# Attention and a two-layer MLP on one core: weight pieces in attention decoded like the others, decoding spread, omega loaded first, layer 2's first sums placed earlier

## The chip, the cores and the metric

The kernel runs on one core of a Trainium2 chip. A core has five engines with a queue of instructions each: TensorE (PE in the profile, with its weight loads as PEld), VectorE (DVE), ScalarE (ACT), GpSimd (POOL) and SyncE (SP), which here only issues DMAs. The metric is the device time of one execution in microseconds (us), the median of several. Lower is better.

## The reference

Inputs are float32 after drawing, but U, V and the two weight matrices come as float64, eight bytes a number.

```python
q_s, k_s = q * scale, k * scale                      # (8, 8, 576, 64), scale = 64 ** -0.25
def phi(x):
    proj = einsum('bhsd,md->bhsm', x, omega)         # omega (128, 64)
    h = proj - sum(x * x, -1, keepdims=True) / 2
    h = h - max(h, -1, keepdims=True)
    return exp(h) / sqrt(128)
kv  = einsum('bhsm,bhsd->bhmd', phi(k_s), v);  z = sum(phi(k_s), 2)
num = einsum('bhsm,bhmd->bhsd', phi(q_s), kv)
den = einsum('bhsm,bhm->bhs', phi(q_s), z) + 1e-6
x = (num / den) as (8, 576, 512)
u = x + ((x^T @ U) @ V)^T                            # mixing over the sequence, rank 32
out = u + relu(u @ w_ch1) @ w_ch2                    # 512 -> 2048 -> 512
```

## The kernel before, in words

Products need nearly full float32 precision, so an operand is split into a high and a low half in float32r (`xh`/`xl`, `wh`/`wl`, `uh`/`ul`, `gh`/`gl`), and three matmuls make one product: high by high, high by low, low by high. The high half is a cast on ACT, the low one a subtraction on DVE or POOL.

**Attention** is a loop of 16 rounds with nine steps each, one step for each tile of 128 positions. A round handles keys of one pair of heads and queries of another at once. A step's stages are delayed against each other over loop iterations (the dictionary DELAY): transposing 384 columns every third step (`xT`, L611, DVE), high and low halves (L615 ACT, L619 POOL), the projection with omega into `p_p` (L738 to L740, PE), the negated maximum `nm` (L746, DVE, one per step), the exponential `e` (L753, ACT, four per step), for keys the sum `p_kv` (L650), for queries a transpose `p_q` (L676), its copy `eT` (L681, in turns on DVE and ACT), the product `p_n` with the keys' sum (L696), and the division (L706 to L721, DVE). Finished sequences go through `mixing`, one piece of which is run twice per loop iteration; it writes `u` to DRAM.

**Decoding.** In the same loop a generator, `decoding`, turns float64 into float32. A piece is 128 rows of up to 512 numbers: a DMA brings the two words of each number into `raw` (two buffers, SP, L192 for weights), ACT takes the magnitude of the high word (L132), and DVE does the rest in slots, one for each call of the generator: clamp (L150), shift (L151) and sign (L154). For the low word there are two ways. The first `lean` pieces take two more DVE slots (L157, L158) that make a correction `de`, which POOL adds in float32 (L176). Later pieces have ACT round the low word to an integer `low` (L135), which POOL adds to the bits (L171). `lean` is EARLY = 11 pieces: U, two of V and eight of the first weight matrix, which is all that the loop decodes but the beginning of a twelfth; `left` allows the loop 64 calls. The loop calls the generator in two of three iterations. At a piece's last slot the next magnitude and a further load are issued. What is done with a decoded piece (`rest`: sums, casts, low halves) is spread over the next piece's slots.

**The MLP** uses Strassen-like products with seven multiplications (S1 to S4 are the sums of the left operand, T1 to T4 of the right one). Layer 1 goes over nine chunks of 512 rows and four weight groups `g`; `unit` does one chunk by one group, seven products `i` of 12 matmuls each (L954). Its results are added on DVE (L942), passed through ACT's relu (L938) and stored to DRAM by SP (L932). An accumulator bank is used again by a later product, so that one waits for the addition that empties the bank. In the last chunk, layer 2's weights are split beside (`w2_ops`, L505 on ACT, L509 on DVE and POOL), and the first left operand of layer 2, `acts[0] = Step(0)`, is prepared: its load (L1130, 1 MB), sums (`value`, L1145; S1 and S3 on POOL, S2 and S4 on DVE) and splits (`split`, L1171 on ACT and L1178 on DVE). S1 to S4 stand in the products 0 to 3 of group 3.

**Layer 2** takes 36 steps of 84 matmuls (L1331). After the first product of its step 0, the pools `up` and `dec` are closed and their memory becomes the pool `vp`, in the order in which its tiles are first asked for: `gh` and `gl` (nine buffers each), then `graw`, which `Step(1)` loads. A tile waits for those readers and writers whose place it takes. Step 1 starts only when all of its seven operands are there (`now.need(6 if n else i)`).

**Order.** Instructions that go through `K` (`keep_in_program_order`) keep the program's order on their engine; that holds for decoding's DVE slots and ACT passes, for the additions of `unit`, and for sums and splits. The others, DMA issues and most of attention's instructions among them, are put in order by the framework's planner, which follows data and a model of the durations. An engine then runs its queue strictly in that order, so a waiting instruction holds up all behind it.

Of the kernel before, what the change touches and what calls it, by code (L numbers as in the profile page):

```python
# [9 lines left out]
F32 = mybir.dt.float32  # L10
F32R = mybir.dt.float32r
U32 = mybir.dt.uint32
I32 = mybir.dt.int32
AF = mybir.ActivationFunctionType
ALU = mybir.AluOpType
# [14 lines left out]
def performer_mlp_kernel(ctx: ExitStack, tc, q, k, v, omega, U, V, w1, w2, out):  # L30
# [7 lines left out]
    nc = tc.nc  # L38
    B, H, S, D = q.shape
# [3 lines left out]
    P = 128  # L43
    NP = B // 2
    NU = H // 2
    NT = 9
# [7 lines left out]
    scale = float(D) ** -0.25  # L54
# [3 lines left out]
    K = tc.keep_in_program_order  # L58
# [26 lines left out]
    warm = const.tile([P, 1], F32, name="warm")  # L85
# [27 lines left out]
            return outer[n // 2][:, n % 2]  # L113
        return dec.tile([P, PIECE, 2], U32, name="raw", bufs=RB)

    def decoding(jobs, late, lean, base, hold=(), defer=()):


        raws, mags, lows = {}, {}, {}
        fetched = [0]  # L120

        def fetch(i):
            while fetched[0] < min(i, len(jobs)):
                j = fetched[0]
                raws[j] = raw_place(j, base)[:, : jobs[j][1], :]
                jobs[j][0](raws[j])
                fetched[0] += 1

        def magnitude(i):
            if i < len(jobs):  # L130
                mags[i] = jobs[i][2]()
                K(nc.scalar.activation(out=mags[i], in_=f32(raws[i][:, :, 1]), func=AF.Abs))  # L132
                if i >= lean:
                    lows[i] = dec.tile([P, PIECE], I32, name="low", tag="de", bufs=2)[:, : jobs[i][1]]
                    K(nc.scalar.activation(out=lows[i], in_=raws[i][:, :, 0], func=AF.Copy, scale=2.0**-29))  # L135

        fetch(depth())
        for _ in range(late):
            yield
        magnitude(0)  # L140
        rest = []
        for i, job in enumerate(jobs):
            n = job[1]
            raw, m = raws.pop(i), mags.pop(i)
            low, high = raw[:, :, 0], raw[:, :, 1]
            e = lows.pop(i) if i in lows else dec.tile([P, PIECE], F32, name="de", bufs=2)[:, :n]


            slots = [
                lambda: nc.vector.tensor_scalar(m, m, _LEAST, _MOST, ALU.max, ALU.min),  # L150
                lambda: nc.vector.tensor_scalar(  # L151
                    words(m), words(m), 3, 0x3FFFFFFF, ALU.logical_shift_left, ALU.bitwise_and
                ),
                lambda: nc.vector.scalar_tensor_tensor(  # L154
                    words(m), high, 0xC0000000, words(m), ALU.bitwise_and, ALU.bitwise_or
                ),
                lambda: nc.vector.tensor_scalar(words(e), words(m), 0xFF800000, None, ALU.bitwise_and),  # L157
                lambda: nc.vector.scalar_tensor_tensor(e, low, 2.0**-52, e, ALU.mult, ALU.mult),  # L158
            ]
            if i >= lean:  # L160
                slots = slots[:3]
            for j, slot in enumerate(slots):
                tc.keep_in_program_order(slot())
                for _ in range(-(-len(rest) // (len(slots) - j))):
                    rest.pop(0)()
                if j == len(slots) - 1 and i not in hold and i not in defer:
                    magnitude(i + 1)
                if j == len(slots) - 1:
                    fetch(i + 1 + depth())
                    if i >= lean:  # L170
                        nc.gpsimd.tensor_tensor(out=m.bitcast(I32), in0=m.bitcast(I32), in1=e, op=ALU.add)  # L171
                yield
            if i in defer:
                magnitude(i + 1)
            if i < lean:
                nc.gpsimd.tensor_tensor(out=m, in0=m, in1=e, op=ALU.add)  # L176
            rest = [lambda fn=fn, m=m: fn(m) for fn in job[3:]]
            if i in hold:
                while rest:
                    rest.pop(0)()  # L180
                    yield
                magnitude(i + 1)
        while rest:
            rest.pop(0)()
            yield
# [128 lines left out]
    def weight_jobs():  # L314
        for g in range(NG):
            yield from w1_jobs(g)
# [55 lines left out]
    EARLY = 1 + 2 + 4 * EARLY_GROUPS  # L372
# [154 lines left out]
    late = {}  # L527
# [53 lines left out]
        spare[:, n : n + 4 * D1].rearrange("p (h b d) -> p h b d", h=2, b=2),  # L581
    ))

    def blocks(src, raw, unit, j):


        pair, hp = unit
        for h in range(2):
            for a in range(2):
                r = h * D + a * BLK  # L590
                nc.sync.dma_start(
                    out=raw[r : r + BLK, j * S : (j + 1) * S].rearrange("i (b c) -> i b c", c=BLK),
                    in_=src[2 * pair + j, 2 * hp + h, :, a * BLK : (a + 1) * BLK].rearrange("(b i) c -> i b c", i=BLK),
                )

    class Part:
# [4 lines left out]
            self.raw = io.tile([P, 2 * S], F32, name=("kt", "qt")[place])  # L601
            self.xh, self.xl = [], []

        def load(self, j):
            blocks(self.src, self.raw, self.unit, j)

        def turn(self):

# [163 lines left out]
    units = [(pair, hp) for pair in range(NP) for hp in range(NU)]  # L772
    keys = [Keys(i, i) for i in range(2)]
    rounds = {0: list(keys)}
    for j in range(2):
        for p in keys:
            p.load(j)
    nc.vector.memset(warm, 0.0)
    nc.scalar.activation(out=warm, in_=warm, func=AF.Exp)

    nc.vector.memset(idle, 0.0)
    for _ in range(12):
        nc.tensor.matmul(ps.tile([P, P], F32, name="p_m", tag="p_m"), idle, idle, start=True, stop=True)
    om = mp.tile([P, 2, D], F32, name="om", tag="y", bufs=2)
    for j in range(2):
        nc.gpsimd.dma_start(out=om[:, j, :], in_=omega)
    make_identity(nc, ident)
    for vt, vm in values:

# [8 lines left out]
    nc.vector.memset(f32(omh), 0.0)  # L798
    nc.vector.memset(f32(oml), 0.0)
    nc.vector.memset(f32(svm), 0.0)  # L800
    nc.vector.tensor_scalar_mul(om, om, scale)
    pom = ps.tile([P, P], F32, name="p_q", tag="p_q", bufs=2)
    nc.tensor.transpose(pom, om.rearrange("p j d -> p (j d)"), ident)
    for j in range(2):
# [10 lines left out]
        "project": 2, "use0": 4, "peak": 3, "combine": 6,  # L815
    }
    steps = {}
    decoder = decoding([u_job(), *v_jobs(), *weight_jobs()], 6, EARLY, -EARLY, defer=(EARLY + 3,))
    mixers = []
    x = None  # L820
    for s in range(NR * NT + 7):
# [28 lines left out]
        at = lambda op: steps.get(s - DELAY[op])  # L850
        for p in at("turn0").group(0) if at("turn0") else []:
            p.turn()
        if s % 3:
            advance(decoder)
        st = at("copy")
        for p in st.queries() if st else []:
# [331 lines left out]
    for n in range(2, len(order)):  # L1188
        c, g = order[n]
        if n == 2:  # L1190
            widen()
        if g == 0:
            while nxt and nxt.step():
                pass
        if n == 4:
            nxt = rights[2] = prepare(2, temps=None)
        elif g == 0 and 1 < c < NCH - 1:
            nxt = rights[c + 1] = prepare(c + 1)
        if n == 6:
            both(nxt)  # L1200
        if n in (6, 7):
            continue
        right = guest if c == 1 else rights[c]
        leaving = n >= 6 and g == NG - 1
        if c == NCH - 1:
            if g == 0:
                for _ in second:
                    pass
                prepare_w2(0)
                prepare_w2(1)  # L1210
                for _ in range(4):
                    w2_ops[0].step(-1)
            if g == 1:
                acts[0] = Step(0)
        for i in unit(c, g, right, banks(n + 1)):
            chores(n, i)
            if c == NCH - 1:
                if g:
                    w2_ops[g - 1].step()
                w2_ops[g].step(i)  # L1220
                w2_ops[g].step(i)
                if i == 2 and 1 < g + 1 < NG:
                    prepare_w2(g + 1)
                if g + 1 < NG and i > 2 + (g > 0):
                    w2_ops[g + 1].step(-1)
                if g + 1 < NG and i == 6:
                    w2_ops[g + 1].step(-1)
                if g == 2 and i % 2:
                    acts[0].split(len(acts[0].ops))
                if g == 2 and i == 6:  # L1230
                    acts[0].need(2)
                if g == 3 and i < 4:
                    acts[0].value(("S1", "S2", "S3", "S4")[i])
            elif nxt:
                for _ in range(2 if leaving else 1):
                    nxt.step(i if leaving else -1)
# [74 lines left out]
    for n in range(NS):  # L1311
# [9 lines left out]
        for i in range(PRODUCTS):  # L1321
# [14 lines left out]
            if n == 0:  # L1336
                if i == 0:
                    while w2_ops[NG - 1].step():
                        pass
                    phase.close()  # L1340
                    decodes.close()
                    late["vp"] = ctx.enter_context(tc.tile_pool(name="vp", reuse_waits="tile", bufs=1))
                    now.split(3)
                    now.split(4)
                    acts[1] = Step(1)
                else:
                    for _ in range(1 + (i > 2)):
                        step = now if len(now.ops) < PRODUCTS else acts[1]
                        if len(step.ops) < PRODUCTS:
                            step.split(len(step.ops))  # L1350
                        if len(now.ops) == PRODUCTS:
                            now.need(6)
            elif n + 1 < NS:
                acts[n + 1].split(i)
# [42 lines left out]
```

## Time and profile before

| | |
|---|---|
| median of 3 runs | 1077.48 us (1076.21 to 1078.4) |
| profiled execution | 1082.14 us, span 1080.4 us, mean granted clock 0.989 |
| PE busy | 1043.0 us, 97% of the span |
| DVE, ACT, POOL busy | 883.6, 611.7, 511.2 us |
| attention | to about 330 us |
| layer 1 | about 336 to 715 us |
| layer 2 | from about 715 us |

A row such as "L746 DVE TENSOR_REDUCE nm<-p_p 128x4 f32<-128x512 f32 x91 | 61.5, 677 | 5.6 <-ACT e L753 2.6" reads: line 746 of the kernel, engine and operation, output and inputs by the program's names, shapes, how many; busy time in us, mean duration in ns; idle time of the engine just before them, and what ended it. In the rows of waits stand the total in us, the number and the longest. In the rows of stretches stand start and end, length, the busy time of PE, PEld, DVE, ACT and POOL (with instructions), the granted PE clock, the busy share of the DMA engines and GB/s. In the timeline the first two numbers are start and duration, and in brackets stands the idle time before, with what ended it. Durations of matmuls include their way through the array; back to back they start every 0.12 us at full clock.

### The profile page before, as it was taken

Reading aid. Unit: us, or ns where it says so; the run is one execution under the profiler, and the core shown is the slowest. Engines: PE = TensorE matmul, PEld = TensorE weight load, DVE = VectorE, ACT = ScalarE, POOL = GpSimd, SP = SyncE. Lnnn points to the kernel's source line nnn. Section 1 sums busy time; section 2 is a strip of 40 time slices with the busy share of each in tenths; the row PEclk is TensorE's granted clock in tenths of the full one; section 3 lists DMA queues with packets and bytes.
Section 4 is the critical chain, followed back from the end, with each engine's and each line's share of the span. In section 5 each row is a group of like instructions: output and inputs, shape, how many; then the busy total and the mean of one; then the engine's idle time right before and its main releaser. Section 6 shows DMA issues by size and latency. Waiting matters only on the chain. (4 is left out here: it accounts for less than half of the span.)

```text
span 1080.4 us, 23909 instructions
## 1 busy us (share of the span) xinstructions
PE 1043.0 (97%) x8497; PEld 1016.6 (94%) x8497; DVE 883.6 (82%) x1531; ACT 611.7 (57%) x1468; POOL 511.2 (47%) x455
## 2 busy tenths in 40 slices
PE   8999999999998889999999999989999999999998
PEld 7898888889987789999999999989999999999998
DVE  3899899988898966666677576669999999999995
ACT  4888878879874545445345354654444444444442
POOL 3446878856433623223323414445744545535543
PEclk8999999999999989999999999999999999999999
DMA  7779587576335764877778856964445455355451
GB/s 129 139 147 167 104 194 156 108 178 121 87 89 127 200 172 114 231 223 176 190 186 194 223 166 200 314 208 141 173 169 166 144 175 167 128 176 167 132 174 47
DMA packets 380408, 175.55 MB, mean 162 GB/s; under 512 B 275553, under 2 KB 353377, under 8 KB 375681
## 3 DMA queue, kind: packets, MB, share of 16 engines
q1 hardware_dynamic: 380224, 173.97, 60.9%
q8 instruction: 67, 1.10, 0.4%
q14 instruction: 53, 0.43, 0.1%
q0 software_dynamic: 64, 0.07, 0.0%
HBM read 110.00 MB, written 63.96 MB: 161 GB/s over the span
## 5 line engine op out<-in xcount | busy, mean ns | idle before, releaser
L753 ACT ACTIVATE e<-p_p,nm 128x128 f32<-128x128 f32 x576 | 166.4, 388 | 34.0 <-DVE nm L746 22.9
L1145 POOL TENSOR_TENSOR gs<-graw 128x512 f32<-128x512 f32 x70 | 104.0, 1489 | 146.5 <-DMA graw<-g 93.8
L1171 ACT CAST gh<-gs 128x512 fp32r<-128x512 f32 x140 | 86.6, 621 | 152.5 <-DVE gs L1145 76.4
L938 ACT ACTIVATE g<-g 128x512 f32<-128x512 f32 x105 | 66.4, 632 | 170.7 <-DVE g L942 93.6
L619 POOL TENSOR_TENSOR xl<-xT,xh 128x384 fp32r<-128x384 f32 x96 | 101.9, 1078 | 112.2 <-ACT xh L615 97.5
L1178 DVE TENSOR_TENSOR gl<-gs,gh 128x512 fp32r<-128x512 f32 x140 | 138.0, 994 | 15.9 <-ACT gh L1171 14.1
L746 DVE TENSOR_REDUCE nm<-p_p 128x4 f32<-128x512 f32 x144 | 97.7, 680 | 20.6 <-PE p_p L740 10.3
L171 POOL TENSOR_TENSOR wf<-wf,low 128x512 int32<-128x512 int32 x24 | 32.4, 1349 | 135.7 <-ACT g L938 123.4
L738 PE MATMUL p_p<-omh,xh 128*128 128x256 f32 x288 | 93.4, 324 | 1.6 <-ACT e L753 1.3
L1256 POOL TENSOR_TENSOR u<-u,p 128x256 f32<-128x256 f32 x72 | 74.8, 1067 | 33.8 <-DVE u L1256 31.2
L1178 DVE TENSOR_TENSOR gl<-graw,gh 128x512 fp32r<-128x512 f32 x107 | 80.7, 769 | 8.9 <-ACT gh L1171 7.8
L1171 ACT CAST gh<-graw 128x512 fp32r<-128x512 f32 x107 | 63.9, 620 | 41.6 <-PE p_p L1331 9.2
L740 PE MATMUL p_p<-omh,xl 128*128 128x256 f32 x288 | 82.3, 286 | 0.1
L696 PE MATMUL p_n<-kv,eT 128*128 128x65 f32 x512 | 74.8, 274 | 7.5 <-DVE eT L681 3.1
L739 PE MATMUL p_p<-oml,xh 128*128 128x256 f32 x288 | 81.9, 284 | 0.0
L1331 PE MATMUL p_p<-wh,gh 128*128 128x256 f32 x288 | 81.1, 282 | 0.0
L1331 PE MATMUL p_p<-wh,gl 128*128 128x256 f32 x288 | 81.0, 281 | 0.0
L1331 PE MATMUL p_p<-wl,gh 128*128 128x256 f32 x288 | 80.9, 281 | 0.0
L696 PEld LDWEIGHTS p_n<-kv,eT 128*128 128x128 f32 x512 | 68.3, 194 | 12.9 <-DVE eT L681 5.5
L1331 PE MATMUL p_q<-wh,gl 128*128 128x256 f32 x276 | 77.7, 282 | 0.8 <-DVE gl L1178 0.8
L1331 PE MATMUL p_q<-wh,gh 128*128 128x256 f32 x276 | 77.8, 282 | 0.4 <-ACT gh L1171 0.4
L954 PE MATMUL p_n<-uh,wh 128*128 128x256 f32 x256 | 73.3, 286 | 4.6 <-DVE g L942 4.5
(271 smaller groups left out, 4058.6 us busy)
## 6 DMA issues: line engine op xcount, KB each, us to landing
graw<-g SPq DMA_DIRECT2D x36, 1024.0 KB, 5.2
g<-g SPq DMA_DIRECT2D x282, 128.0 KB, 2.4
raw<-in_moe_w_ch_dram SPq DMA_DIRECT2D x22, 512.0 KB, 4.7
u_dram<-ut SPq DMA_DIRECT2D x36, 256.0 KB, 2.4
u<-u_dram SPq DMA_DIRECT2D x36, 256.0 KB, 2.6
out_dram<-u SPq DMA_DIRECT2D x36, 256.0 KB, 2.9
kt<-in_k_dram SPq DMA_DIRECT2D x120, 72.0 KB, 2.7
qt<-in_q_dram SPq DMA_DIRECT2D x120, 72.0 KB, 2.7
```

Source lines behind the costliest of these rows:

```text
L619: nc.gpsimd.tensor_tensor(out=self.xl[-1], in0=self.turned, in1=f32(self.xh[-1]), op=ALU.subtract)
L696: nc.tensor.matmul(pn[:, h, :], eT[:, h, :], kv[:, h, s // 5, :], start=True, stop=True)
L738: nc.tensor.matmul(o, part.xh[g][:, ts], oh, start=True, stop=False)
L739: nc.tensor.matmul(o, part.xh[g][:, ts], ol, start=False, stop=False)
L740: nc.tensor.matmul(o, part.xl[g][:, ts], oh, start=False, stop=True)
L746: nc.vector.tensor_reduce(out=self.nm[:, :n], in_=self.pp[:, :n], axis=AX.X, op=ALU.max, negate=True)
L753: nc.scalar.activation(out=self.e[:, j, :], in_=self.pp[:, j, :], func=AF.Exp, bias=self.nm[:, j : j + 1])
L1145: K(engine.tensor_tensor(out=to, in0=self.val[x], in1=self.val[y], op=op))
L1171: K(nc.scalar.copy(out=h, in_=v))
L1178: K(nc.vector.tensor_tensor(out=l, in0=v, in1=f32(h), op=ALU.subtract))
L1256: K(engine.tensor_tensor(out=out, in0=x, in1=y, op=ALU.add))
L1331: K(nc.tensor.matmul(acc[bank][:, half, :], x[:, ks], y[:, f, :], start=(now.s == 0 and k == 0 and half == 0 and x is h and y is wh), stop ...
```

## The change

Four edits go in at once.

1. `lean` becomes 0: the eleven pieces in attention too take three DVE slots, the low word is rounded on ACT (L135) and added by POOL as an integer. A new argument, `wide = EARLY`, leaves those pieces five calls of the generator, the last two without a DVE step; POOL's add comes after the third.
2. From step 54 on the loop calls the generator in every second iteration, not in two of three.
3. At the start omega is loaded first, once, by SP; the multiplication by `scale` writes it into both halves of `om`. Before, POOL loaded it twice. One of the four first key loads is issued on ACT's queue, behind its first exponential.
4. Layer 2's first sums are taken at products 0, 2 and 4 of group 2 (S1, S3, S2) and product 0 of group 3 (S4). `Step(1)` is created before the two splits that used to come ahead of it, so `graw` is the first tile of the pool `vp`.

```diff
-    def decoding(jobs, late, lean, base, hold=(), defer=()):
+    def decoding(jobs, late, lean, base, hold=(), defer=(), wide=0):
...
             if i >= lean:
                 slots = slots[:3]
+            if i < wide:
+                slots += [None] * (5 - len(slots))
             for j, slot in enumerate(slots):
-                tc.keep_in_program_order(slot())
+                if slot:
+                    tc.keep_in_program_order(slot())
...
                 if j == len(slots) - 1:
                     fetch(i + 1 + depth())
-                    if i >= lean:
-                        nc.gpsimd.tensor_tensor(out=m.bitcast(I32), in0=m.bitcast(I32), in1=e, op=ALU.add)
+                if i >= lean and (j == 2 if i < wide else j == len(slots) - 1):
+                    nc.gpsimd.tensor_tensor(out=m.bitcast(I32), in0=m.bitcast(I32), in1=e, op=ALU.add)
...
-    def blocks(src, raw, unit, j):
+    def blocks(src, raw, unit, j, queue=None):
...
-                nc.sync.dma_start(
+                (queue or nc.sync).dma_start(
...
-    for j in range(2):
-        for p in keys:
-            p.load(j)
+    once = mp.tile([P, D], F32, name="once", tag="y", bufs=2)
+    nc.sync.dma_start(out=once, in_=omega)
     nc.vector.memset(warm, 0.0)
-    nc.scalar.activation(out=warm, in_=warm, func=AF.Exp)
+    K(nc.scalar.activation(out=warm, in_=warm, func=AF.Exp))
+    keys[0].load(0)
+    keys[1].load(0, nc.scalar)
+    for p in keys:
+        p.load(1)
...
-    for j in range(2):
-        nc.gpsimd.dma_start(out=om[:, j, :], in_=omega)
...
-    nc.vector.tensor_scalar_mul(om, om, scale)
+    for j in range(2):
+        nc.vector.tensor_scalar_mul(om[:, j, :], once, scale)
...
-    decoder = decoding([u_job(), *v_jobs(), *weight_jobs()], 6, EARLY, -EARLY, defer=(EARLY + 3,))
+    decoder = decoding([u_job(), *v_jobs(), *weight_jobs()], 6, 0, -EARLY, defer=(EARLY + 3,), wide=EARLY)
...
-        if s % 3:
+        if s % (3 if s < 6 * NT else 2):
             advance(decoder)
...
-                if g == 3 and i < 4:
-                    acts[0].value(("S1", "S2", "S3", "S4")[i])
+                early_sum = {(2, 0): "S1", (2, 2): "S3", (2, 4): "S2", (3, 0): "S4"}.get((g, i))
+                if early_sum:
+                    acts[0].value(early_sum)
...
+                    acts[1] = Step(1)
                     now.split(3)
                     now.split(4)
-                    acts[1] = Step(1)
```

More of the change, by code (lines that the diff above doesn't have):

```diff
@@ L602, in __init__, with load @@
             self.xh, self.xl = [], []
-        def load(self, j):
-            blocks(self.src, self.raw, self.unit, j)
+        def load(self, j, queue=None):
+            blocks(self.src, self.raw, self.unit, j, queue)
         def turn(self):
```

## The prediction

> **What bounds the kernel now.** I read the page first: busy time by engine, then the slices.
>
> ```profile
> span 1080.4 us, 23909 instructions
> ...
> PE 1043.0 (97%) x8497; PEld 1016.6 (94%) x8497; DVE 883.6 (82%) x1531; ACT 611.7 (57%) x1468; POOL 511.2 (47%) x455
> ...
> PE   8999999999998889999999999989999999999998
> ...
> DVE  3899899988898966666677576669999999999995
> ```
>
> PE is busy nearly throughout, so only PE's pauses and its slow clock can be won back. They sit in three places: the first slice, attention (the first dozen slices, DVE at 8 to 9), and the slice near 710 us. Each has its own limit, so I read them apart, attention first, in two stretches: one with the decoding of weights in it, one just after it.
>
> ```profile
> core 0: us, PE busy (x) PEld busy (x) DVE busy (x) ACT busy (x) POOL busy (x), PEclk, DMA share, GB/s
> 33.00:236.00 203.00, 189.56 (x1508) 175.59 (x1506) 188.92 (x439) 169.22 (x547) 138.54 (x137) 0.99 0.73 149
> 236.00:306.00 70.00, 70.00 (x601) 68.28 (x600) 61.41 (x154) 60.74 (x198) 34.99 (x33) 1.00 0.50 107
> ```
>
> Without decoding PE never stops (70.00 of 70). With it DVE is 93% busy (188.92 of 203), ACT 83%, and PE's busy time hides pauses. The loop's steps are counted by the maximum over p_p, one per step; the groups of DVE and ACT in the first stretch, and that one row from the second:
>
> ```profile
> L746 DVE TENSOR_REDUCE nm<-p_p 128x4 f32<-128x512 f32 x91 | 61.5, 677 | 5.6 <-ACT e L753 2.6 <-PE p_p L740 1.8 <-ACT sv L357 0.3
> ...
> L154 DVE SCALAR_TENSOR_TENSOR wf<-raw,wf 128x512 uint32<-128x512 uint32 x9 | 9.0, 1001 | 0.0
> ...
> L150 DVE TENSOR_SCALAR wf<-wf 128x512 f32<-128x512 f32 x9 | 8.2, 914 | 0.1
> ...
> L158 DVE SCALAR_TENSOR_TENSOR de<-raw,de 128x512 f32<-128x512 uint32 x8 | 7.9, 983 | 0.0
> L157 DVE TENSOR_SCALAR de<-wf 128x512 uint32<-128x512 uint32 x8 | 7.7, 969 | 0.0
> ...
> L132 ACT ACTIVATE wf<-raw 128x512 f32<-128x512 f32 x10 | 6.9, 690 | 2.5 <-DMA raw<-in_moe_w_ch_dram 2.5
> ...
> L151 DVE TENSOR_SCALAR wf<-wf 128x512 uint32<-128x512 uint32 x9 | 6.5, 722 | 0.1
> ...
> L135 ACT ACTIVATE low<-raw 128x512 int32<-128x512 uint32 x2 | 1.4, 690 | 0.0
> ```
>
> ```profile
> L746 DVE TENSOR_REDUCE nm<-p_p 128x4 f32<-128x512 f32 x36 | 24.6, 683 | 5.4 <-ACT e L753 1.6 <-ACT eT L681 1.5 <-PE p_p L740 1.4
> ```
>
> A step takes 203/91 = 2.23 us with decoding and 70/36 = 1.94 us without. Both stretches have a mixer running in somewhat over half of their steps, so the difference, 0.287 us x 91 = 26.1 us, is what decoding costs attention. That is the pool to draw from.
>
> **Part 1: three DVE steps for each piece in place of five.** Removed are L157 and L158 of eleven pieces: eight of 512 columns, and U (320) and V (twice 288), by width 1.75 more, 9.75 in all. A piece costs DVE 0.914 + 0.722 + 1.001 + 0.969 + 0.983 = 4.59 us now; 1.95 of that goes, 9.75 x 1.95 = 19.0 us. Added on ACT is one L135 pass per piece, 0.690, together 6.7 us. POOL keeps one add of the same size per piece, on integers and two slots earlier.
>
> Price: 26.1 us pays for 9.75 pieces of 4.59 us of DVE and 0.690 of ACT (L132), 51.5 us together, so 0.507 us for each us of engine time (the casts and POOL's work of a piece, left out here, make this a high price). DVE's part is -9.6. Bounds: 0 if PE waits for latency and not for DVE's throughput, -19.0 if each us of DVE counts in full. I take the price, since DVE is the busiest helper but not always the one that PE waits for. From the waits of that stretch, the engines' and then SP's own (us in total, times, longest):
>
> ```profile
> PE p_n L696 <- DVE eT L681: 3.1, 8, 1.0
> ...
> PE p_n L696 <- ACT eT L681: 2.7, 2, 1.8
> ...
> ACT wf L132 <- DMA raw<-in_moe_w_ch_dram: 2.5, 2, 1.9
> ```
>
> ```profile
> SPq L192 <- DVE de L158: 4.6, 5, 1.3
> ```
>
> The first two rows name both engines. For ACT's 6.7 us the bounds are 0 and +6.7, the same price gives +3.4; I take +2.0, because ACT idles 17% where DVE idles 7%. Queued behind the new pass on ACT are the step's eT copies and exponentials, for which PE waits. Cover for it is that idle share; without it the whole 6.7 returns.
>
> The last two rows are a side effect. A raw buffer is freed by its last reader, L158 in slot five today and L154 in slot three afterwards. SP stood 4.6 us at the head of its queue for L158, and ACT 2.5 us for a late raw load, with the exponentials behind it. I count -0.6 (bounds 0 and -2.5).
>
> **Part 2: decoding spread.** The first 36 of the 64 advances keep their steps; the other 28 take every second step instead of two of three, 56 steps in place of 42. About 7 of them move into the stretch where DVE has 8.6 us of idle in 70. Their number and order stay. Worth -0.4, between -1.5 and +0.5. Attention together: -9.6 + 2.0 - 0.6 - 0.4 = -8.6.
>
> **Part 3: the start.** The chain at the start ends with the last of four key loads, not with omega:
>
> ```profile
> 7.13 2.12 SPq L591 DMA_DIRECT2D qt<-in_k_dram  x4
> ...
> 11.53 0.58 DVE L611 STREAM_TRANSPOSE xT<-qt 128x384 f32<-128x384 f32 x1 [1.49 <-DMA qt<-in_k_dram]
> ```
>
> ```profile
> 2.00:8.00 6.00, 5.64 (x16) 3.61 (x16) 1.78 (x6) 1.10 (x5) 2.45 (x15) 1.00 0.91 147
> ```
>
> One group of four issues (2.12 us) goes from SP to ACT, idle then, and one omega load (I price it as a quarter of such a group, 0.53) comes ahead on SP, so SP gets to the last group 1.6 us sooner; value loads follow in that queue and gain the same. POOL loses two issues. But the DMA engines are already 0.91 busy, which allows 9% of some 9 us. I take -0.8, between -1.6 and +0.5 (keys behind omega). One multiplication becomes two halves in DVE's idle time: nothing.
>
> **Part 4: into layer 2.** First the chain of waits, then DVE and POOL in the timeline, PE's waits, and the clock after them:
>
> ```profile
> 707.09 1.10 DVE wl L509
> 708.19 1.67 DVE uraw L1145
> 709.86 0.61 DVE g L942
> ...
> 710.51 4.63 PE p_n L954 x24
> ...
> 717.82 6.78 DMA graw<-g
> ```
>
> ```profile
> 704.70 1.78 DVE L509 TENSOR_TENSOR wl<-ts,wh 128x512 fp32r<-128x512 f32 x1
> ```
>
> ```profile
> 704.19 1.74 POOL L1145 TENSOR_TENSOR uraw<-graw 128x512 f32<-128x512 f32 x1
> ...
> 707.61 1.71 POOL L1145 TENSOR_TENSOR graw<-graw 128x512 f32<-128x512 f32 x1
> ```
>
> ```profile
> PE p_n L954 <- DVE g L942: 5.2, 4, 2.1
> ```
>
> ```profile
> 711.16:714.57 3.41, 3.41 (x18) 3.41 (x18) 2.71 (x5) 3.01 (x6) 1.29 (x1) 0.50 0.44 121
> ```
>
> PE waits 2.1 us for the addition g at 709.86. Ahead of it in DVE's fixed order stands S2 (L1145, 1.67), beside POOL's S1 and S3 (1.74, 1.71). The new order puts S1, S3 and S2 into the weight group before, and leaves S4 ahead, priced at 0.6 like the addition of its shape. The addition then starts some 1.7 - 0.6 + 0.6 = 1.7 earlier, the last 0.6 estimated from what DVE's 1.78 and 1.10 lose without S1 and S3 beside them: -1.7 of the 2.1 (bounds 0 and -2.1). Behind the pause stand 3.41 us at half clock, 1.7 us lost; I take -1.5 (0 to -1.7).
>
> The Trainium skill ("TensorE: Matmul & The Clock Gate", What's actually happening) says that the clock falls to half after at least one idle window of about 3.4 us. Here 2.1 us of pause stood ahead of it, and the row decides; by the page the pause wouldn't be the cause, the 1.5 would fall away, and the total below would be 1065.4.
>
> Then the load of Step(1):
>
> ```profile
> 712.00 5.73 SPq L932 DMA_DIRECT2D g<-g  x8
> 717.82 0.42 SPq L1130 DMA_DIRECT2D graw<-g  x1
> ```
>
> ```profile
> 725.35 0.39 PE L1331 MATMUL p_q<-wh,gh 128*128 128x256 f32 x1 [0.38 <-ACT gh L1171]
> 726.64 0.38 PE L1331 MATMUL p_q<-wh,gl 128*128 128x256 f32 x1 [0.78 <-DVE gl L1178]
> ```
>
> It is issued behind eight stores and lands at 724.6, and PE pauses 0.38 + 0.78 = 1.16. Created first, graw takes the front of the new pool, where raw stood (the wl at 707.09 is its last reader on DVE), instead of operands that PE reads until 715.14, the end of its x24 row. If SP's order still has the stores ahead, nothing changes; if not, all 1.16 goes. I take -1.0, since a load with nothing to wait for should pass stores that wait. gh and gl move onto places that earlier work has left. Layer 2 together: -1.7 - 1.5 - 1.0 = -4.2.
>
> **Sum.** -8.6 - 0.8 - 4.2 = -13.6. The profiled execution took 1082.14 us around its span of 1080.4, 4.7 above the median of the runs; the difference is taken off the median: 1077.5 - 13.6 = **1063.9**.
>
> **The rivals.**
>
> *ACT takes DVE's place.* After the forecast, ACT would be at (169.2 + 6.7)/194.4 = 90%, DVE at (188.9 - 19.0)/194.4 = 87%. For it: PE waits for ACT's eT as for DVE's. Against it: ACT passed 87% in the free stretch without holding PE. If 87% is ACT's ceiling, the stretch takes 202 and attention gains nothing: 1077.5 - 5.0 = 1072.5.
>
> *DVE counts in full.* For it: 93% busy. Against it: PE's named waits for DVE are small. -19.0 in attention, -1.6 and -4.9 elsewhere: 1052.
>
> *Layer 2 keeps its pause.* S1 to S3 disturb the group before as they disturb this one. There DVE has idle time:
>
> ```profile
> 691.00 0.69 DVE L942 TENSOR_TENSOR g<-p_n,u 128x512 f32<-128x512 f32 x1 [2.27 <-DMA g<-g]
> ...
> 700.40 0.69 DVE L942 TENSOR_TENSOR g<-p_kv,u 128x512 f32<-128x512 f32 x1 [1.41 <-DMA g<-g]
> ```
>
> The 3.7 us hold S2 (1.67) and two stretched neighbours. Should they not, part 4 is lost: 1068.1.
>
> *Slower: ACT's two passes in a row open pauses that halve the clock.* L132 and L135 together hold the exponentials up by 1.38 us, and a pause of PE of 1.0 (the eT row) stood ahead of this:
>
> ```profile
> 48.97:52.38 3.41, 3.41 (x19) 3.41 (x18) 2.68 (x7) 3.23 (x11) 1.99 (x2) 0.50 0.63 141
> ```
>
> Price 0.69 + 1.7 = 2.39 a piece, 19.1 for the eight wide ones; with the 2.0 for ACT taken back, 1063.9 - 2.0 + 19.1 = 1081.0. It decides from the seventh piece on (15.6/2.39 = 6.5). Against it: a pause of 1.8 (the ACT eT row) halved nothing.
>
> *The sums and steps move and PE doesn't notice* (latency bounds attention, the group before takes layer 2's pause): the start alone, 1076.7.
>
> **How the numbers follow.** Forecast 0.50; layer 2 keeps its pause 0.10; DVE in full 0.10; ACT's ceiling 0.13; unnoticed 0.08; slower 0.09. The forecast's own range is 1059 to 1069. The range 1055 to 1075 holds the first, the second and ACT's ceiling, and the near half of DVE in full; unnoticed and slower lie outside it. Under 0.2% (2.2 us) can't be told from no change. Faster 0.83, same 0.08, slower 0.09.
>
> **What would show it.** Steps near 2.1 us between 33 and 236 us, ACT at or above 88% there, and the waits of ACT for raw gone; the first maximum before 12.1 us; no half clock near 710, S4 alone ahead of the addition, and graw landed before its predecessor's products end. The forecast is wrong if ACT heads PE's waits, or if the layer 2 pause only changes its group.

## The result and the profile after

The changed kernel took 1070.02 us (median of 5 runs, 1066.44 to 1071.95) against 1077.48 for the kernel before on the same chip: a ratio of 0.9924, 95% interval 0.9907 to 0.9940. That is 7 to 8 us, a little over half of the 13.6 that was forecast.

The profiled execution took 1071.45 us. First its page, busy time by engine:

```profile
span 1069.5 us, 23886 instructions
...
PE 1036.0 (97%) x8497; PEld 1013.1 (95%) x8497; DVE 867.7 (81%) x1510; ACT 614.5 (57%) x1479; POOL 504.1 (47%) x453
```

DVE's busy time fell by 15.9 us and ACT's rose by 2.8. So the change did take time off DVE; what became of it is what the experiments ask.

PE runs the same 8497 products in every kernel of this study, inside attention at some places in another order. I cut at three products ahead of which the same products stand in every trace, so that the time between two cuts can be compared: one near the end of attention (before: 309.39 us), one in the last chunk of layer 1 (702.44), one in layer 2's steady part (755.80). From the last cut to the start of PE's last product every trace takes 320.62 us.

| profiled execution | attention | layer 1 | entry to layer 2 |
|---|---|---|---|
| before | 309.39 | 393.04 | 53.36 |
| after | 305.85 | 389.52 | 49.66 |
| difference | -3.5 | -3.5 | -3.7 |

Layer 1's 3.5 is nothing of the change's: before had 6.8 us of half clock from 383.5 on, 3.4 us lost, that after did not have; another of 3.4 us near 328 they both have. So attention gave 3.5 where 9.4 were forecast (8.6 and the start's 0.8), and the entry 3.7 where 4.2 were.

The two stretches of attention in the changed kernel, and two short stretches inside (busy time of PE, PEld, DVE, ACT and POOL, granted clock, DMA share, GB/s); then the step maximum, counted in the two long stretches, and the new ACT pass:

```profile
33.00:236.00 203.00, 193.53 (x1567) 183.05 (x1567) 177.71 (x427) 174.36 (x566) 130.86 (x136) 0.98 0.75 151
236.00:306.00 70.00, 67.96 (x565) 66.09 (x565) 59.57 (x149) 59.58 (x193) 36.59 (x36) 0.98 0.47 102
84.27:91.10 6.83, 6.75 (x33) 6.75 (x34) 3.97 (x9) 4.35 (x16) 1.97 (x2) 0.50 0.76 120
241.30:244.70 3.40, 3.40 (x20) 3.40 (x19) 1.78 (x5) 2.26 (x8) 0.94 (x2) 0.50 0.92 226
```

```profile
L749 DVE TENSOR_REDUCE nm<-p_p 128x4 f32<-128x512 f32 x94 | 64.0, 681 | 16.0 <-PE p_p L743 10.1 <-ACT e L756 1.7 <-ACT xh L618 1.6
...
L135 ACT ACTIVATE low<-raw 128x512 int32<-128x512 uint32 x9 | 6.2, 694 | 0.0
```

```profile
L749 DVE TENSOR_REDUCE nm<-p_p 128x4 f32<-128x512 f32 x34 | 23.2, 682 | 6.0 <-PE p_p L743 2.8 <-ACT eT L684 1.5 <-ACT e L756 1.1
```

A step takes 203/94 = 2.16 us in the first stretch (2.23 before) and 70/34 = 2.06 in the second (1.94 before). Together that is 128 steps in place of 127: the first stretch's gain is nearly paid back in the second. DVE fell from 188.9 to 177.7 us of the 203, ACT rose from 169.2 to 174.4. Both engines now have idle time, and yet PE stops: two of its pauses are followed by the half clock of the third and fourth row.

Here is the first. ACT's timeline and PE's one row:

```profile
81.79 0.66 ACT L132 ACTIVATE wf<-raw 128x512 f32<-128x512 f32 x1 [1.19 <-DMA raw<-in_moe_w_ch_dram]
82.36 0.64 ACT L135 ACTIVATE low<-raw 128x512 int32<-128x512 uint32 x1
82.90 0.35 ACT L684 COPY eT<-p_q 128x256 f32<-128x256 f32 x1
```

```profile
83.31 0.44 PE L699 MATMUL p_n<-kv,eT 128*128 128x65 f32 x2 [2.10 <-ACT eT L684]
```

ACT stands 1.19 us at a magnitude pass whose raw load lands late, then does the new pass, and only then the copy `eT` that PE needs. PE is idle for 2.10 us, and 6.83 us at half clock follow. The second:

```profile
236.80 0.74 ACT L250 CAST wh<-wf 128x256 fp32r<-128x256 f32 x2
237.42 0.70 ACT L132 ACTIVATE wf<-raw 128x512 f32<-128x512 f32 x1
237.99 0.68 ACT L135 ACTIVATE low<-raw 128x512 int32<-128x512 uint32 x1
238.55 0.52 ACT L618 CAST xh<-xT 128x384 fp32r<-128x384 f32 x1
238.95 0.39 ACT L684 COPY eT<-p_q 128x256 f32<-128x256 f32 x1
239.21 1.69 ACT L756 ACTIVATE e<-p_p,nm 128x128 f32<-128x128 f32 x6
```

```profile
239.99 0.63 PE L699 MATMUL p_n<-kv,eT 128*128 128x65 f32 x4 [2.04 <-ACT e L756]
```

ACT is never idle here: casts, magnitude, low words and a cast again stand in a train of 2.2 us ahead of `eT`. These are single places; averaged over the stretch, ACT is at 86%. And neither comes of edit 1. The kernel before has the first pause too, 1.82 us at 83 us, with no pass L135 there, behind a longer wait of ACT for the load:

```profile
82.45 0.66 ACT L132 ACTIVATE wf<-raw 128x512 f32<-128x512 f32 x1 [1.91 <-DMA raw<-in_moe_w_ch_dram]
```

The second stands at a piece after the eleven of edit 1, and such pieces take L135 in the kernel before as well (its row of x2). It was the spread that moved this one here: `e7_spread_only` below, which has no edit 1, has the same two passes at 238.2 us and a pause of 0.95 behind them.

### The profile page after: what moved, and what is told of

It reads as the page before. It is cut to its first block, busy times and chain, and to the rows that moved or that the text cites. A ratio compares the mean times of both kernels' runs of the same rounds, so it can differ in the third digit from the quotient of the medians.

```text
span 1069.5 us, 23886 instructions
## 1 busy us (share of the span) xinstructions
PE 1036.0 (97%) x8497; PEld 1013.1 (95%) x8497; DVE 867.7 (81%) x1510; ACT 614.5 (57%) x1479; POOL 504.1 (47%) x453
## 5 line engine op out<-in xcount | busy, mean ns | idle before, releaser
L622 POOL TENSOR_TENSOR xl<-xT,xh 128x384 fp32r<-128x384 f32 x96 | 97.0, 1027 | 113.0 <-ACT xh L618 101.6
L1183 DVE TENSOR_TENSOR gl<-gs,gh 128x512 fp32r<-128x512 f32 x140 | 134.8, 971 | 15.4 <-ACT gh L1176 13.6
L174 POOL TENSOR_TENSOR wf<-wf,low 128x512 int32<-128x512 int32 (+2 forms) x35 | 45.1, 1289 | 141.3 <-ACT g L943 120.6
L1337 PE MATMUL p_q<-wl,gh 128*128 128x256 f32 x276 | 77.5, 281 | 0.0
```

The costliest lines, as they stand in the source:

```text
L622: nc.gpsimd.tensor_tensor(out=self.xl[-1], in0=self.turned, in1=f32(self.xh[-1]), op=ALU.subtract)
L1183: K(nc.vector.tensor_tensor(out=l, in0=v, in1=f32(h), op=ALU.subtract))
L1337: K(nc.tensor.matmul(acc[bank][:, half, :], x[:, ks], y[:, f, :], start=(now.s == 0 and k == 0 and half == 0 and x is h and y is wh), stop ...
```

## The experiments

Ratios are to the kernel before on the same chip, with 95% intervals; 0.001 is 1.08 us.

### Edit 1 alone, and its two halves

`e1_pieces` is the kernel before with edit 1 (the line of the call; the rest stands in the change's diff):

```diff
-    decoder = decoding([u_job(), *v_jobs(), *weight_jobs()], 6, EARLY, -EARLY, defer=(EARLY + 3,))
+    decoder = decoding([u_job(), *v_jobs(), *weight_jobs()], 6, 0, -EARLY, defer=(EARLY + 3,), wide=EARLY)
```

> The kernel before with edit 1 alone: the eleven pieces in attention take three DVE slots and one more ACT pass. Theory (a price for each us of engine time): DVE's 19.0 us are worth -9.6 and ACT's 6.7 us +2.0, with -0.6 for earlier raw loads: 8.2 us under the kernel before, steps near 2.14 us between 33 and 236 us. Rival (trains of ACT passes and late raw loads open pauses that halve PE's clock): 2 to 4 us under it, with half clock in the decoding stretch where the kernel before has none. Rival (PE waits for latency, DVE's time is free): within 1 us.

Measured: 1083.63 us, 1.0046 (1.0027 to 1.0066). Five us slower, where the forecast had a clear gain. Its profiled execution was its quickest (1075.05, granted clock 0.992); the others had 0.983 to 0.989 and took 1080.8 to 1085.8.

`e2_dve_only` takes the ACT pass away again: the low words are left out, and POOL adds a tile of noughts (the two lines that matter):

```diff
+                if i < wide:
+                    lows[i] = nought[0][:, : jobs[i][1]]
```

> Edit 1 without its ACT pass: the low words are left out, POOL adds a tile of noughts instead, so DVE's two steps go and nothing comes on ACT. Theory (price): 10.2 us under the kernel before. Rival (trains of ACT passes): 8 to 10 us under it, so the same, but then the kernel with edit 1 whole is 4 us or more slower than this one. Rival (DVE's time is free): within 1 us of the kernel before. Rival (DVE counts in full): 17 to 19 us under it.

Measured: 1080.04, 1.0015 (0.9998 to 1.0032). With DVE's two steps gone and nothing put on ACT, nothing is gained. So it was not ACT alone that ate the gain. With the ACT pass besides, `e1_pieces` is 3.3 us slower by the ratios, little more than the noise.

This nothing is a sum, though. The mean granted clock was 0.9865 over the runs of `e2_dve_only` and 0.9867 over those of `e1_pieces`, against 0.9908 for the kernel before on the same chip. As (1 - clock) x span that is 14.6 and 14.4 us against 9.9. In the profile of `e2_dve_only` two half-clock stretches begin where PE had stood for 2.65 us and where it stood for 4.41:

```profile
125.03:131.85 6.82, 6.82 (x34) 6.64 (x33) 4.13 (x10) 3.76 (x12) 4.80 (x5) 0.50 0.26 79
193.29:203.53 10.24, 7.67 (x36) 7.49 (x36) 7.54 (x16) 3.63 (x12) 4.66 (x5) 0.50 0.46 74
```

Nor did DVE get 19 us back: it was busy for 876.8 us there against 883.6 before, since clamps stood beside POOL for up to 5.93 us (last section). So something was gained and lost again; how much of each was not measured apart.

`e3_act_only` is the kernel before with the added ACT pass into a tile that nobody reads:

```diff
+                if i < lean:
+                    K(nc.scalar.activation(out=aside, in_=raws[i][:, :, 0], func=AF.Copy, scale=2.0**-29))
```

> The kernel before with the ACT pass added to each of the eleven pieces, its result unused, and the two DVE steps kept. Theory (price, ACT idle 17% of that stretch): 2.0 us over the kernel before, at most 3.4. Rival (trains of ACT passes open pauses): 5 to 10 us over it. Rival (ACT's time is free): within 1 us.

Measured: 1077.54, 1.0000 (0.9986 to 1.0014). The pass is free as long as pieces keep five DVE slots.

### The spread: alone, with edit 1, and further

`e7_spread_only` is the kernel before with edit 2 alone:

```diff
-        if s % 3:
+        if s % (3 if s < 6 * NT else 2):
```

> Edit 2 alone, on five DVE slots. Theory I: 0.4 us under the kernel before, within 1.5. Theory III: 3 to 10 us under it. Theory IV (edits 1 and 2 need each other: the free slots pay only where the passes stand further apart): within 2 us of the kernel before, while both together are 4 us or more under it.

Measured: 1073.12, 0.9971 (0.9956 to 0.9986), 3 us faster. `e5_pieces_spread` has edits 1 and 2.

> Edits 1 and 2 together on the kernel before (three DVE slots, and from step 54 every second step). Edit 1 alone was 5 us over the kernel before. Theory I (the price of engine time, with the half clock as an accident of where pauses fall): 4 to 8 us under the kernel before. Theory II (edit 1 brings nothing that PE sees; what the whole change gains comes from the start and layer 2): 3 to 6 us over it. Theory III (edit 2 is what attention gains by, edit 1 a ballast): 1 to 5 us under it, and then edit 2 alone is better than both together.

Measured: 1071.57, 0.9956 (0.9935 to 0.9977). Against `e7_spread_only` edit 1 adds nothing that can be told; against `e1_pieces` the spread is worth 9 to 10 us. Edit 1 alone is a loss that the spread removes.

`f3_third` is the changed kernel with one call in three from step 54 on. `f4_third_five` has the same rhythm and edits 3 and 4, but five DVE slots.

```diff
-        if s % (3 if s < 6 * NT else 2):
+        if s % 3 if s < 6 * NT else s % 3 == 1:
```

> The changed kernel, with decoding called at every third step from step 54 on, in place of every second: its 28 calls end near step 137, in place of 109. Theory of call density: the loss per step with a call falls further, and the later steps, which have no decoding now, give back some of it; 2 to 4 us less than 1070, so 1066 to 1068. Theory of the forecast (a price per us of engine time, spread worth 0.4): no change, within 1.5. If spreading only moves the cost to later steps: no change or up to 2 more.

> As f3_third, but with five VectorE steps for a piece and no ACT pass for its low words, that is, the kernel before with the spread at every third step, the new start and the new order of layer 2. Theory of call density: three slots or five make no difference, so the same as f3_third within 1.5. Theory of the forecast: 7 to 8 us more than f3_third, since 19.0 us of VectorE come back and 6.7 us of ACT go.

Measured: 1071.95, 0.9945 (0.9925 to 0.9965), and 1071.38, 0.9932 (0.9914 to 0.9950). Neither is better than its sibling at every second step, the changed kernel and `e8_no_pieces` below. So the loss doesn't fall on in step with the density of calls: my theory for this pair fell. The two are alike, so at this rhythm too edit 1 is worth nothing.

### The change without edit 1

`e8_no_pieces` has edits 2, 3 and 4, whose lines stand in the change's diff.

> The whole change without edit 1: edits 2, 3 and 4 on five DVE slots. Theory I: 4 to 6 us under the kernel before, so 2 to 4 us slower than the whole change. Theories II and III: as fast as the whole change or faster, 7 to 14 us under the kernel before. Theory IV: 2 to 5 us under the kernel before.

Measured: 1068.95, 0.9932 (0.9913 to 0.9952), against the changed kernel's 0.9924 (0.9907 to 0.9940). Edit 1 could be left out of the change, and no difference would be measured. What edit 1 does to PE's waits shows between 33 and 310 us (total, times, longest), first of `e8_no_pieces`, then of the changed kernel, which differ by edit 1 alone:

```profile
PE p_n L696 <- DVE x L721: 4.0, 4, 1.2
PE p_n L696 <- DVE eT L681: 1.7, 5, 0.4
PE p_q L676 <- ACT e L753: 1.3, 2, 1.0
PE p_p L738 <- ACT e L753: 1.3, 7, 0.2
PE p_n L696 <- ACT eT L681: 0.8, 1, 0.8
```

```profile
PE p_q L679 <- ACT e L756: 3.3, 3, 1.3
PE p_n L699 <- ACT eT L684: 2.9, 3, 2.1
PE p_n L699 <- ACT e L756: 2.0, 1, 2.0
PE p_p L741 <- ACT e L756: 1.4, 8, 0.2
PE p_n L699 <- DVE x L724: 0.6, 1, 0.6
```

In the rows shown, the waits that name DVE fall from 5.7 to 0.6 us, and those that name ACT rise from 3.4 to 9.6. PE's waits changed their name and grew fewer and longer. That the sum is larger is not the price of edit 1: these two executions lie further apart (1066.54 and 1071.45 us) than the kernels do.

### Single stalls

Two kernels leave the engines' work as it is in the changed kernel and move one thing each. `f1_fetch_early` issues the next raw load at a wide piece's third slot, where the buffer comes free, and not at the fifth:

```diff
-                if j == len(slots) - 1:
+                if j == (2 if i < wide else len(slots) - 1):
                     fetch(i + 1 + depth())
```

> The changed kernel, with the load of the next raw piece issued at a wide piece's third slot, two calls sooner than now (the raw buffer is free from there). Theory of single pauses: the pause of 2.1 us at 81.2 us of the changed kernel, where ACT stood 1.19 us for a raw load, and the half clock from 84.3 to 91.1 behind it go away; 2 to 4 us less than the changed kernel's 1070, so 1066 to 1068. Theory of call density (what counts is how many steps of the loop carry a call of the decoding): no change, 1070 within 1.5. Theory of the forecast (a price per us of engine time): the same engine time, no change beyond the 0.6 named there.

Measured: 1066.99, 0.9889 (0.9871 to 0.9907). `f2_low_later` moves the low words' pass one call later, out of the train, for all wide pieces but the first:

```diff
-                    K(nc.scalar.activation(out=lows[i], in_=raws[i][:, :, 0], func=AF.Copy, scale=2.0**-29))
+                    if not 0 < i < wide:
+                        K(nc.scalar.activation(out=lows[i], in_=raws[i][:, :, 0], func=AF.Copy, scale=2.0**-29))
...
+                if j == 0 and 0 < i < wide:
+                    K(nc.scalar.activation(out=e, in_=low, func=AF.Copy, scale=2.0**-29))
```

> The changed kernel, with the ACT pass for a wide piece's low words moved one call later, so that the two ACT passes of a piece no longer stand in a row. Theory of single pauses by ACT's train: the pause of 2.0 us at 237.95 us and the half clock behind it (241.3 to 244.7) go away; 2 to 4 us less than 1070. Theory of call density: no change, 1070 within 1.5. The prediction's slower rival (two passes in a row halve the clock): up to several us less.

Measured: 1066.43, 0.9885 (0.9867 to 0.9903). By the ratios they are 3.8 and 4.2 us faster than the changed kernel. The first one's interval meets that of the changed kernel at its end, the second's ends just short of it, and the two were not timed on the chip of the changed kernel, so the size is rougher than the sign. Both are the quickest kernels of this study. They were not put together. ACT's timeline at the place of the first pause, of `f1_fetch_early` and then of `f2_low_later`; between them the first one's stretch in which the changed kernel was at half clock:

```profile
79.04 0.70 ACT L132 ACTIVATE wf<-raw 128x512 f32<-128x512 f32 x1
79.61 0.67 ACT L135 ACTIVATE low<-raw 128x512 int32<-128x512 uint32 x1
80.17 0.38 ACT L684 COPY eT<-p_q 128x256 f32<-128x256 f32 x1
```

```profile
84.27:91.10 6.83, 6.83 (x64) 6.83 (x63) 6.80 (x18) 6.07 (x22) 2.20 (x3) 1.00 0.81 112
```

```profile
80.70 0.67 ACT L132 ACTIVATE wf<-raw 128x512 f32<-128x512 f32 x1 [0.43 <-DMA raw<-in_moe_w_ch_dram]
81.27 0.36 ACT L687 COPY eT<-p_q 128x256 f32<-128x256 f32 x1
```

In the one the load is there when ACT comes to it; in the other ACT still waits, 0.43 us, but `eT` follows at once. PE's pause there shrank from 2.10 us to 0.83 in the first and to 0.33 in the second, and no half clock follows. But the changed kernel's own code can do that too. Up to about 130 us `f3_third` has the same instructions in the same order on every engine; in its trace ACT did not wait for that load, no half clock followed, and PE's row was:

```profile
82.86 0.66 PE L699 MATMUL p_n<-kv,eT 128*128 128x65 f32 x4 [0.46 <-ACT eT L684]
```

So the pause of 2.1 us and its half clock belong to one execution, and from which places the 3.8 and 4.2 us come stays open. The other half of what I expected of `f2_low_later` did not come. The train at 238 us belongs to a piece that is no longer wide, its pass stayed, and the pause there was 1.58 us with 3.4 us of half clock behind it.

### The start and layer 2

`e6_start` has edit 3 alone, `e4_layer2` edit 4 alone, with the lines of the change's diff.

> Edit 3 alone (omega first on SP, one key load on ACT's queue). Forecast of the start: 0.8 us under the kernel before. Rival (the start also moves the half clock that follows the first pauses, 14.8 to 21.7 us in the profile of before): 2 to 5 us under it, with a higher mean granted clock. Rival (nothing): within 0.5 us.

Measured: 1075.85, 0.9991 (0.9975 to 1.0006): not to be told from nothing. But the rival saw something: the mean granted clock of its runs was 0.9935 against 0.9908. In the seven traces without edit 3 a half-clock stretch of 3.4 to 10.2 us begins between 14 and 17 us; in the seven with it none begins before 28 us. Without the edit PE pauses near 14 us for 1.2 to 2.0 us, with it for 0.6 at most.

> The kernel before with edit 4 alone: S1 to S3 in the weight group before, and graw first in the new pool. Theory: the pause of 2.1 us near 708 us, the half clock behind it and the 1.16 us near 725 us go: 4.2 us under the kernel before. Rival (the group before takes the pause): 0 to 1 us under it, with a pause of PE in group 2.

Measured: 1075.60, 0.9978 (0.9964 to 0.9993), some 2.3 us. The traces say why that is less than the 3.7 of the profiled pair. Between the last two cuts, the kernels with the old order of layer 2 took 50.0 to 50.9 us (`e1`, `e2`, `e3`, `e5`, `e6`, `e7`; mean 50.4), those with the new one 48.6 to 49.7 (seven; mean 49.3), and only the profiled execution of before took 53.36. PE's row at the same place in `e7_spread_only`, with the old order:

```profile
702.50 0.38 PE L954 MATMUL p_n<-uh,wh 128*128 128x256 f32 x1 [1.11 <-DVE g L942]
```

The pause that the profile of before showed as 2.1 us is 1.1 in five of these six traces and 1.99 in `e2_dve_only`, and no half clock follows it: in none of the other traces is there any near 710 us. With the new order the four kernels with edit 1 took 49.6 to 49.7 us, the three without it 48.6 to 48.9; the cause of that stays open.

## Why the prediction was right and wrong

**Direction.** Faster was right, by steps other than the main one. 1070.0 lies in the range of 1055 to 1075, and outside the forecast's own 1059 to 1069. That it lies in the range at all is luck in part: the 8.2 us of part 1 did not come, and the spread, priced at 0.4, made up for some of them.

**Part 1, DVE -9.6: the step that failed.** Its price, 0.507 us for each us of engine time, took the 26.1 us that decoding costs attention for a toll on engine time. `e2_dve_only` took DVE's two steps away for nothing (1.0015), and the pairs at equal rhythm (the changed kernel and `e8_no_pieces`, `f3_third` and `f4_third_five`, `e5_pieces_spread` and `e7_spread_only`) show the same without that kernel's gap in the arithmetic. The 19.0 us that the price was applied to were mis-sized as well. The mean 0.969 and 0.983 us of L157 and L158 were taken beside POOL; where POOL does nothing beside them they take 0.41 and 0.67 (3 and 9 cases in the seven traces that have them), so an estimate of their own time is 9.75 x 1.08 = 10.5 us. DVE's busy time fell by 6.4 to 12.7 us in the five pairs of profiles that differ in these steps. The lower bound that stood there, 0, was met. Its reason, that PE waits for latency and not for DVE's throughput, is not shown, since the clock took time back in `e1_pieces` and `e2_dve_only`. What the runs do show is that here the order in the queues was worth more than engine time: `f1_fetch_early` and `f2_low_later` change no engine's work and gain more than edit 1.

**ACT +2.0:** 0.0 by `e3_act_only`, with five slots. With three slots the 3.3 us between `e1_pieces` and `e2_dve_only` are near the term and its price of 3.4, but rough. The two places shown above, where the pass stands ahead of `eT`, are not this cost: edit 1 made neither.

**Earlier raw loads, -0.6 (bound -2.5):** mis-sized, and not reached by the change. The buffer does come free at slot three, but the load is still issued at slot five. SP's wait at L158 is gone, as was said, but ACT's wait for the load is not: 1.19 us at 81 us in that execution (1.91 before, 0 in `f3_third`). Issuing the load where the buffer comes free gained 3.8, beyond the bound; that it did so by this one pause is not shown.

**Part 2, spread -0.4 (-1.5 to +0.5):** mis-sized. It is worth 3 us alone (0.9971), and the whole interval of `e7_spread_only`, -1.5 to -4.7, lies at or outside the bound. I had taken it for a shift of the same cost to later steps. By the starts of the step maximum, steps 54 to 99 fell from 104.0 to 96.5 us in that kernel, steps 99 to 117 rose from 34.0 to 36.4. That calls in two steps in a row are what costs, which the old rhythm has and the new ones don't, would fit both the gain and the missing further gain of one call in three; it was not tested apart.

**Part 3, start -0.8:** the first maximum came at 12.07 us, 12.14 before. 0.9991 is compatible with the 0.8 and with nothing. That the change moves the half clock near 15 us was not in the sum.

**Part 4, -4.2:** the right place and mechanism, about twice the size. The pause for the addition is gone, and so is the half clock; but its 2.1 us and the half clock behind it, 1.5 of the sum, were those of one execution. Nor is the entry free of pauses now. ACT's waits in the changed kernel between 690 and 740 us, and the chain of waits there:

```profile
ACT gh L1176 <- DMA g<-g: 2.9, 1, 2.9
```

```profile
707.67 2.45 DMA g<-g
...
710.22 0.63 ACT gh L1176
...
711.62 2.90 PE p_kv L1337 x22
```

The prediction let `gh` and `gl` move onto places that earlier work has left. One `gh` got a place that a store of layer 1 was still reading, and PE paused 1.0 us for it (in `e4_layer2` 0.2).

**The rivals.** "ACT takes DVE's place" was nearest in time (1072.5), and its sign came true: ACT heads PE's waits, which the prediction had named as what would show it wrong. But its mechanism, a ceiling at 87% of ACT, is not what the traces show, since the same ACT work in another order was quicker (`f2_low_later`). "DVE in full" fell with `e2_dve_only` and with `e8_no_pieces`. "Layer 2 keeps its pause" was half right. The slower rival, two ACT passes in a row that open pauses and halve the clock, has its half clock in the runs of `e1_pieces`, but not its cause: `e2_dve_only`, without the second pass, has the same clock, and the places at 81 and 238 us do not come of edit 1. "Unnoticed" fell: the spread was noticed.

## What to carry to other kernels

Where PE is at 95% and its helpers at 85%, don't price a helper's work by the us: list PE's pauses of over a us, find for each what stood in the queue ahead of the instruction that PE needed, and move that. A step's busy time beside another engine can be waiting in part: price it by what it takes where the other does nothing. An edit that lets a buffer go earlier brought no load forward here; the load's issue has to move with it. A pause or a half clock that one profile shows belongs to that execution until a second trace of the same code shows it too; other variants' traces of an untouched stage serve for that, as `f3_third` did here.

## What the hardware did that I had not expected

**A clamp on DVE that waits for POOL.** In the changed kernel one clamp (L150), which takes 0.43 us or less where POOL does nothing beside it, took 3.03. POOL's timeline, then DVE's, ACT's and PE's rows, all of the changed kernel:

```profile
124.70 1.98 POOL L622 TENSOR_TENSOR xl<-xT,xh 128x384 fp32r<-128x384 f32 x2
126.64 1.28 POOL L401 TENSOR_TENSOR ml<-x,mh 128x512 fp32r<-128x512 f32 x1
127.88 0.73 POOL L255 TENSOR_TENSOR wl<-wf,wh 128x256 fp32r<-128x256 f32 x1
```

```profile
125.85 3.03 DVE L150 TENSOR_SCALAR wf<-wf 128x512 f32<-128x512 f32 x1
128.81 0.68 DVE L749 TENSOR_REDUCE nm<-p_p 128x4 f32<-128x512 f32 x1
```

```profile
129.60 1.14 ACT L756 ACTIVATE e<-p_p,nm 128x128 f32<-128x128 f32 x4 [2.41 <-DVE nm L749]
```

```profile
130.02 0.33 PE L679 MATMUL p_q<-ident,e 128*128 128x128 f32 x1 [1.33 <-ACT e L756]
```

POOL's work runs without a gap to 128.61, and the clamp ends 0.28 us later; behind it the maximum, the exponentials and PE are late, PE by 1.33. In `e2_dve_only` it is worse. POOL, DVE and PE there:

```profile
191.49 2.50 POOL L407 TENSOR_TENSOR ml<-x,mh 128x512 fp32r<-128x512 f32 x2
```

```profile
188.34 5.93 DVE L156 TENSOR_SCALAR wf<-wf 128x512 f32<-128x512 f32 x1
```

```profile
195.86 1.12 PE L705 MATMUL p_n<-kv,eT 128*128 128x65 f32 x4 [4.41 <-DVE eT L690]
```

POOL was busy from 181.14 to 193.99; the clamp ended at 194.27, again 0.28 later, and PE stood 4.41 us. In all fourteen traces each clamp and shift of over 1.2 us ended 0.28 to 0.29 us after an instruction of POOL. Of over 2 us there was one or more in each of the seven traces with edit 1, none in the seven without it. In these executions that is a part of where edit 1's gain went; how much of the 5 us that it costs alone was not measured apart. It isn't a rule without exception: in `e8_no_pieces` a clamp at 122.34 us took 0.45 between two instructions of such a train. The Trainium skill ("SBUF — State Buffer", SBUF: two separate sides) says that VectorE in some modes and GpSimd share a pair of ports as an exclusive lock, held for a whole instruction, with the loser fully blocked. The rows agree with the blocking; here it lasted over several instructions of POOL, not one.

**Half clock after short pauses, in pieces of one length.** All half-clock stretches in the clock records ahead of the end lasted 3.41 us or a multiple. In the changed kernel pauses of 2.10 and 2.04 us stood ahead of one, in `f1_fetch_early` one of 1.57; pauses of 1.33 and 1.08 in the changed kernel, of 1.82 at 83 us before and of 1.99 near 708 us in `e2_dve_only` had none behind them, yet one of 1.00 at 26 us, with one of 0.58 next to it, had one 2.6 us later, so length alone doesn't decide. The mean granted clock differed between runs of one kernel, in `e1_pieces` from 0.983 to 0.992. Over 117 runs of thirteen kernels, within a kernel, a run went 0.55 us longer for each us that (1 - clock) x span was larger, so the clock is part of the spread, and one profile of 1070 us is good for a stage to about 3 us, by my estimate.
